# Three padding tiles ahead of the tiles that the tensor engine reads

## The chip, the cores and the metric

The kernel runs on one core of a Trainium2 chip. The metric is the device time of one execution in microseconds (us); the median of a few executions counts. On that core TensorE (PE in the profile) multiplies, with its weight loads listed apart as PEld. VectorE (DVE) and ScalarE (ACT) do the elementwise work, GpSimd (POOL) and SyncE (SP) mostly issue DMAs. A tile lies in the on-chip memory (SBUF) as 128 partitions, and its place is the byte address at which it begins in each partition.

## The reference

```python
q_s = softmax(q, axis=-1)                      # b=8, h=8, s=576, d=64, with 1e-9 in the divisor
k_s = softmax(k, axis=2)                       # over the sequence
kv  = einsum('bhsd,bhse->bhde', k_s, v)
x   = einsum('bhsd,bhde->bhse', q_s, kv)       # then laid out as 4608 tokens x 512
gate = sigmoid(x @ w_gate)                     # 512 x 1536
out  = (gate * (x @ w_val)) @ w_out            # 1536 x 512
```

Linear attention, then a gated feed-forward layer over 4608 tokens, all in float32.

## The kernel before

The tokens are cut in nine windows of 512 (`w` = 0 to 8). Window 0 is computed with plain float32 products (lines 594 and 621) while the weights arrive, are converted, and are cut in a high and a low part. Windows 1 to 8 run in six stages each (`p` = 0 to 5), 48 stages in all, and a stage is `g1(w, p)` and, one stage late, `g2` of the stage before.

`g1` (line 629) forms gate and value of 256 hidden columns with a Strassen-like scheme: seven products `prod`, each of 12 matmuls (two halves `n`, two pieces `kt`, and three pairs of parts: high by high, high by low, low by high). The stationary operand, which the weight load reads, is either `a_w` (the weights, products A11, A12, A22) or `s_sb` (sums of the weights, products S1 to S4). The moving operand is always `c_hl`, 256 columns. So a stage has 36 matmuls with `a_w` and 48 with `s_sb`, all on line 639, all 128x128 by 128x256 in the `float32r` type:

```python
        prod(y, wa(A11), B11, True, False)
        nc.scalar.copy(out=sg[:, 0], in_=y)
        prod(z, wsum(S1), T1, True, False)
        nc.scalar.copy(out=sg[:, 2], in_=z)
        more(S1)
        prod(y, wsum(S2), T2, False, False)
```

`a_w` stays in SBUF for all windows. `s_sb` is one tile: each of its quarters is read by a product, and is then filled again from DRAM by a DMA that GpSimd issues (line 260). `g2` (line 694, matmuls on line 702) multiplies `h` (stationary) by `wo_hl` (moving, 512 columns), 24 matmuls in a stage, and sums over the six stages of a window in PSUM; `wo_hl` too is loaded again in each stage (line 208).

The attention of the next window is woven into the stages: `k_mm` (line 362, plain float32) in stage 2, and `x_mm` (line 522) in stage 4, which multiplies `kv_sb` (stationary) by `ring` tiles (moving). `x_mm` has the same triples of parts as `prod`, and cuts its 512 columns in two where a window crosses from one batch to the next, so that its matmuls have 64 to 512 columns.

The order of the instructions on each engine is that in which the code is written (`tc.manual_schedule()`). Tiles get their places by pools, one after the other in the order in which pools are opened, and within a pool in the order in which tags are first used:

```python
    const = ctx.enter_context(tc.tile_pool(name="const", bufs=1))
    apool = ctx.enter_context(tc.tile_pool(name="apool", bufs=1))
    two = ctx.enter_context(tc.tile_pool(name="two", bufs=2))
    four = ctx.enter_context(tc.tile_pool(name="four", bufs=4))
    ring = ctx.enter_context(tc.tile_pool(name="ring", bufs=11))
```

The first pool, `const`, starts behind some small constants at byte 1152, which is 128 past a multiple of 512. Its big tiles, and the two `kt` tiles of 2304 bytes together, are multiples of 512 long, so they keep that remainder (only the second `kt`, which TensorE does not read, has another), and so does `ident`, 512 bytes long. Behind `ident` come four small tiles (`q_m`, `kmax_0`, `q_r`, `k_r0`: 320 bytes with their rounding), after which `apool` and `two` start with the remainder 448. The last tiles of `two` are six small ones (`k_max`, `k_neg`, `k_sum`, 192 bytes), after which `four` and `ring` have the remainder 128 again.

| tile | read by | role | start, remainder by 512 bytes |
|---|---|---|---|
| `s_sb` | L639 | stationary | 128 |
| `a_w` | L639 | stationary | 448 |
| `c_hl` | L639 | moving | 448 |
| `h` | L702 | stationary | 448 |
| `wo_hl` | L702 | moving | 448 |
| `kv_sb` | L522 | stationary | 128 |
| `ring` | L522 | moving | 128 (384 for a cut at an odd multiple of 64 columns) |

Every slice that these lines take of their tiles starts a multiple of 512 bytes behind the tile's start, but for the cut `ring` slices of the last row.

Of the kernel before, what the change touches and what calls it, by code (L numbers as in the profile page):

```python
# [8 lines left out]
F32 = mybir.dt.float32  # L9
# [8 lines left out]
P = 128  # L18
# [33 lines left out]
def attn_moe(ctx: ExitStack, tc: tile.TileContext, qf, qn, qT, k, kT, v, wg, wv, wo, out):  # L52
    nc = tc.nc

    const = ctx.enter_context(tc.tile_pool(name="const", bufs=1))
    apool = ctx.enter_context(tc.tile_pool(name="apool", bufs=1))
    two = ctx.enter_context(tc.tile_pool(name="two", bufs=2))
    four = ctx.enter_context(tc.tile_pool(name="four", bufs=4))
    ring = ctx.enter_context(tc.tile_pool(name="ring", bufs=11))
    dpool = ctx.enter_context(tc.tile_pool(name="dpool", bufs=2, space=bass.MemoryType.DRAM))  # L60
# [2 lines left out]
    ps_gv = ctx.enter_context(tc.tile_pool(name="ps_gv", bufs=3, space=bass.MemoryType.PSUM))  # L63
    ps_at = ctx.enter_context(tc.tile_pool(name="ps_at", bufs=1, space=bass.MemoryType.PSUM))

    s_sb = const.tile([P, 4, 2, 2, 2 * P], F32R, name="s_sb")
    x_32 = const.tile([P, NP, T], F32, name="x_32")
    sg = const.tile([P, 4, 2, HT], F32, name="sg")
# [12 lines left out]
    )  # L81
    ident = const.tile([P, P], F32, name="ident")
    make_identity(nc, ident)

    ctx.enter_context(tc.manual_schedule())

# [992 lines left out]
```

## Time and profile before

| | us |
|---|---|
| median of 3 runs | 1014.23 (1014.09 to 1016.1) |
| profiled execution, its own time | 1016.99 |
| its span, first to last instruction | 1015.2 |
| PE busy | 957.5 (94%) |
| PEld busy | 826.2 (81%) |
| DVE busy | 611.1 (60%) |
| ACT busy | 475.9 (47%) |

The profiled execution's own time is 1.8 us over its span, and 2.8 us over the median of the runs. In a list by time the first column is the start, the second the time to the group's last end. Matmuls overlap, so one of them lasts far longer (some 280 ns) than the distance to the next; what a matmul costs is that distance, which is the start of the next group less the start of this one, divided by the count. That distance is called the pitch below.

### The profile page before, as it was taken

The numbers are of one execution on the slowest core, as the hardware profiler recorded it, in microseconds if no ns is written. First come the engines' busy times: TensorE is split into PE (matmuls) and PEld (weight loads), VectorE is DVE, ScalarE is ACT, GpSimd is POOL, SyncE is SP. The second block draws the span as 40 slices with busy tenths as digits, with TensorE's granted clock in tenths as the row PEclk, the third lists the DMA queues.
The fourth block names the chain that finished last, engine by engine and source line by source line (L and its number), as shares of the span: only waits on it lengthen the run. The fifth ranks groups of instructions, "written<-read, shape, count | busy, mean of one in ns | idle before, by whom it ended". The sixth has DMA issues, their size and how long they took to land.

```text
span 1015.2 us, 15663 instructions
## 1 busy us (share of the span) xinstructions
PE 957.5 (94%) x6062; PEld 826.2 (81%) x6062; DVE 611.1 (60%) x1010; ACT 475.9 (47%) x815; POOL 171.2 (17%) x323
## 2 busy tenths in 40 slices
PE   5959899878899999999999999999999999999998
PEld 4525344468799999999999999999999999999997
DVE  8476967566266656666666656665665475464342
ACT  3639887345154535363446344633463344353222
POOL 0000001121112211211122111211221122212120
PEclk8979999979799999999999999999999999999999
DMA  9837756889569996899699968996999679868672
GB/s 334 320 106 272 267 222 172 309 266 339 153 207 208 371 322 205 230 365 313 199 248 358 310 200 262 353 300 203 277 340 275 214 203 340 244 184 249 205 208 83
DMA packets 94873, 259.88 MB, mean 256 GB/s; under 512 B 15376, under 2 KB 17680, under 8 KB 94160
## 3 DMA queue, kind: packets, MB, share of 16 engines
q0 software_dynamic: 44720, 170.42, 54.7%
q1 hardware_dynamic: 50080, 88.48, 29.3%
q8 instruction: 48, 0.79, 0.4%
q14 instruction: 25, 0.20, 0.1%
HBM read 230.29 MB, written 28.56 MB: 255 GB/s over the span
## 4 chain that ended last, share of the span: by engine, by line
PE 76%; DMA 8%; ACT 8%; DVE 5%; issue 3%; POOL 1%; SPq 0%; POOLq 0%; DVEq 0%; ACTq 0%
PE gv L639 43%; PE acc L702 22%; PE gv L594 3%; PE at L362 3%; DMA kmax_row<-k_max 2%; PE acc L621 2%; PE gv L522 2%; ACT ring L341 1%; DMA s<-s_sb 1%; ACT ring L441 1%; DMA q_m_row<-q_m 1%; DMA ring<-v_in 1%; DMA ring<-qT_in 1%; ACT kt L295 1%; DMA q_b<-q_m_row 1%
## 5 line engine op out<-in xcount | busy, mean ns | idle before, releaser
L639 PE MATMUL gv<-c_hl,s_sb 128*128 128x256 f32 x2304 | 283.0, 278 | 12.3 <-ACT sg L657 12.2
L639 PEld LDWEIGHTS gv<-c_hl,s_sb 128*128 128x128 f32 x2304 | 272.5, 189 | 14.7 <-ACT sg L657 14.1
L702 PE MATMUL acc<-wo_hl,h 128*128 128x512 f32 x1152 | 272.8, 393 | 0.0
L702 PEld LDWEIGHTS acc<-wo_hl,h 128*128 128x128 f32 x1152 | 214.7, 189 | 43.7 <-issue 0.2
L639 PE MATMUL gv<-c_hl,a_w 128*128 128x256 f32 x1728 | 231.9, 284 | 0.0
L639 PEld LDWEIGHTS gv<-c_hl,a_w 128*128 128x128 f32 x1728 | 220.2, 192 | 4.1 <-issue 1.0
L260 POOL DMA_DIRECT2D s_sb<-s x192 | 102.2, 533 | 327.1 <-PE gv L639 321.5
L665 DVE TENSOR_TENSOR sg<-gv,sg 128x512 f32<-128x512 f32 x48 | 33.2, 691 | 177.7 <-PE gv L639 177.7
L208 POOL DMA_DIRECT2D wo_hl<-wo x96 | 51.1, 533 | 310.4 <-PE acc L702 307.7
L594 PE MATMUL gv<-x,f_w 128*128 128x512 f32 x160 | 72.7, 607 | 9.5 <-ACT h L602 5.6
L667 ACT COPY sg<-gv 128x512 f32<-128x512 f32 x48 | 28.2, 587 | 107.0 <-PE gv L639 107.0
L657 ACT COPY sg<-gv 128x512 f32<-128x512 f32 x48 | 28.0, 584 | 97.7 <-PE gv L639 73.3
L594 PEld LDWEIGHTS gv<-x,f_w 128*128 128x128 f32 x160 | 30.4, 194 | 47.4 <-issue 34.4
L669 DVE TENSOR_TENSOR sg<-sg 128x512 f32<-128x512 f32 x48 | 33.2, 693 | 57.1 <-ACT sg L667 57.1
L621 PE MATMUL acc<-wo_t,h 128*128 128x512 f32 x96 | 47.3, 639 | 14.1 <-DVE h L606 14.1
L690 DVE TENSOR_TENSOR h<-sg,h 128x1024 fp32r<-128x1024 f32 x48 | 58.8, 1226 | 1.6
L672 ACT ACTIVATE sg<-sg 128x512 f32<-128x512 f32 x48 | 30.4, 632 | 54.0 <-DVE sg L671 54.0
L678 DVE TENSOR_TENSOR sg<-sg 128x512 f32<-128x512 f32 x48 | 33.2, 693 | 33.5 <-ACT sg L672 33.5
L621 PEld LDWEIGHTS acc<-wo_t,h 128*128 128x128 f32 x96 | 19.3, 205 | 40.4 <-issue 23.8
L662 ACT COPY sg<-gv 128x512 f32<-128x512 f32 x48 | 28.2, 587 | 44.4 <-PE gv L639 44.4
L659 ACT COPY sg<-gv 128x512 f32<-128x512 f32 x48 | 28.1, 586 | 26.1 <-PE gv L639 26.0
L396 ACT CAST kv_sb<-kmax_b 64x256 fp32r<-64x256 f32 x14 | 5.7, 404 | 66.5 <-DVE kmax_b L372 66.1
(155 smaller groups left out, 1056.1 us busy)
## 6 DMA issues: line engine op xcount, KB each, us to landing
s_sb<-s POOLq DMA_DIRECT2D x192, 512.0 KB, 7.1
wo_hl<-wo POOLq DMA_DIRECT2D x96, 512.0 KB, 5.7
s<-s_sb POOLq DMA_DIRECT2D x5, 2048.0 KB, 8.1
out<-x SPq DMA_DIRECT2D x36, 256.0 KB, 8.8
ring<-k_in SPq DMA_DIRECT2D x28, 256.0 KB, 14.3
ring<-qn_in SPq DMA_DIRECT2D x28, 256.0 KB, 10.4
q_b<-q_m_row SPq DMA_DIRECT2D x56, 128.0 KB, 8.7
ring<-qT_in SPq DMA_DIRECT2D x28, 256.0 KB, 9.0
```

The costliest lines, as they stand in the source:

```text
L208: nc.gpsimd.dma_start(out=t.rearrange("p h e -> p (h e)"), in_=wo_dram[2 * p + i].bitcast(F32R))
L260: nc.gpsimd.dma_start(out=s_sb[:, i].rearrange("p h n e -> p (h n e)"), in_=s_dram[p][:, i * n:(i + 1) * n].bitcast(F32R),)
L362: nc.tensor.matmul(kvps[b][:, hp], lhsT=kt[:n, sl], rhs=vt[:n, sl], start=(t == 0 and hp == 0), stop=(t == len(KTILES) - 1 and hp == NP - ...
L594: nc.tensor.matmul(ps[n], lhsT=w[:, kt // 2, sl], rhs=x_0[:, kt], start=(kt == 0), stop=(kt == NK - 1),)
L621: nc.tensor.matmul(acc[0][m], lhsT=h_0[j][:, m * P:(m + 1) * P], rhs=wo_t[j // 2][:, j % 2], start=(j == 0), stop=(j == NJ - 1),)
L639: nc.tensor.matmul(ps[:, n], lhsT=lh(kt), rhs=c_hl[i][:, x, kt], start=(first and n == 0 and kt == 0 and lh is wh and x == 0), stop=(last ...
L665: nc.vector.tensor_tensor(out=sg[:, 0], in0=rr, in1=sg[:, 0], op=ALU.add)
L669: nc.vector.tensor_tensor(out=sg[:, 3], in0=sg[:, 3], in1=sg[:, 2], op=ALU.add)
L672: nc.scalar.activation(sg[:, 0:2, 0], sg[:, 0:2, 0], AF.Sigmoid)
L678: tt(out=sg[:, 0:2, 0], in0=sg[:, 0:2, 0], in1=sg[:, 0:2, 1], op=ALU.mult)
L690: nc.vector.tensor_tensor(out=lo, in0=sg[:, :, 0], in1=hi.bitcast(F32), op=ALU.subtract)
L702: nc.tensor.matmul(acc[w][m], lhsT=h[lh][:, i, sl], rhs=o[i][:, rh], start=(p == 0 and i == 0 and lh == 0 and rh == 0), stop=(p == NS - 1 ...
```

## The change

```diff
@@ attn_moe
     two = ctx.enter_context(tc.tile_pool(name="two", bufs=2))
+    pad = ctx.enter_context(tc.tile_pool(name="pad", bufs=1))
+    pad.tile([P, 80], F32, name="pad_2")
     four = ctx.enter_context(tc.tile_pool(name="four", bufs=4))
...
+    const.tile([P, 96], F32, name="pad_0")
     s_sb = const.tile([P, 4, 2, 2, 2 * P], F32R, name="s_sb")
...
     make_identity(nc, ident)
+    const.tile([P, 48], F32, name="pad_1")
```

Nothing reads or writes the new tiles. `pad_0` has 384 bytes and stands ahead of `s_sb`: 128 + 384 = 512, so the tiles of `const` start at remainder 0. `pad_1` has 192 bytes and joins the 320 of the small tiles: 320 + 192 = 512, so `apool` and `two` start at remainder 0. `pad_2` has 320 bytes and joins the 192 at the end of `two`: 192 + 320 = 512, so `four` and `ring` start at remainder 0. All tiles of the table above then have the remainder 0 (the cut `ring` slices 256). Each engine has the same instructions in the same order as before, with the same waits; the addresses alone differ. Lines behind the pool list move down by 2 to 5 (line 639 becomes 644, line 702 becomes 707).

## Prediction

> **What bounds the kernel now.** I read the page's busy times first, then the main loop alone by windows, then what PE waited for there.
>
> ```profile
> span 1015.2 us, 15663 instructions
> PE 957.5 (94%) x6062; PEld 826.2 (81%) x6062; DVE 611.1 (60%) x1010; ACT 475.9 (47%) x815; POOL 171.2 (17%) x323
> ...
> 400.00:500.00 100.00, 99.45 (x708) 93.04 (x707) 63.10 (x105) 46.31 (x86) 19.16 (x36) 1.00 0.96 277
> 500.00:600.00 100.00, 99.57 (x714) 93.29 (x713) 63.63 (x107) 46.33 (x86) 19.16 (x36) 1.00 0.97 281
> ...
> PE gv L639 <- ACT sg L657: 2.1, 5, 0.4
> ```
>
> In the windows the columns are PE, PEld, DVE, ACT and POOL busy, the granted clock, the DMA share and GB/s. PE is busy for 99.5 of 100 us at a full clock, and the last row, from the waits after 300 us, has 2.1 us in all for which PE stood still. So the loop is bound by PE's stream of matmuls, and a nanosecond more or less in each is paid in full. DMA engines are 96% occupied, but nothing waits for them in that loop beyond those 2.1 us.
>
> What does a matmul cost? One undisturbed stage in the list by time of PE:
>
> ```profile
> 945.03 1.60 PE L639 MATMUL gv<-c_hl,a_w 128*128 128x256 f32 x12
> 946.47 2.88 PE L639 MATMUL gv<-c_hl,s_sb 128*128 128x256 f32 x24
> 949.19 1.60 PE L639 MATMUL gv<-c_hl,a_w 128*128 128x256 f32 x12
> 950.63 2.88 PE L639 MATMUL gv<-c_hl,s_sb 128*128 128x256 f32 x24
> 953.35 1.60 PE L639 MATMUL gv<-c_hl,a_w 128*128 128x256 f32 x12
> 954.79 5.63 PE L702 MATMUL acc<-wo_hl,h 128*128 128x512 f32 x24
> 960.25 1.60 PE L639 MATMUL gv<-c_hl,a_w 128*128 128x256 f32 x12
> ```
>
> From start to start: 12 matmuls with `a_w` take 1.44 us, 120 ns each; 24 with `s_sb` take 2.72 us, 113.3 ns each; 24 on line 702 take 5.46 us, 227.5 ns each. The stage takes 15.22 us. The reader is to see the first two numbers: the same line, shape, type and moving tile, yet 6.7 ns apart. Both stationary slices are 128 contiguous words of the same layout. What differs is where they start: `s_sb` at remainder 128 of 512 bytes, `a_w` at 448, against `c_hl` at 448. The means in the page's groups say the same less sharply:
>
> ```profile
> L639 PE MATMUL gv<-c_hl,s_sb 128*128 128x256 f32 x2304 | 283.0, 278 | 12.3 <-ACT sg L657 12.2
> L639 PE MATMUL gv<-c_hl,a_w 128*128 128x256 f32 x1728 | 231.9, 284 | 0.0
> ```
>
> A third pair of tiles tells which property counts. `x_mm` reads `kv_sb` at 128 and `ring` at 128, here once in pieces of 256 and once of 512 columns:
>
> ```profile
> 500.31 2.31 PE L522 MATMUL gv<-ring,kv_sb 128*128 128x256 f32 x18
> 502.46 0.88 PE L522 MATMUL at<-ring,kv_sb 128*128 128x256 f32 x6
> 503.18 1.59 PE L639 MATMUL gv<-c_hl,a_w 128*128 128x256 f32 x12
> ...
> 896.43 2.21 PE L522 MATMUL gv<-ring,kv_sb 128*128 128x512 f32 x9
> 898.48 0.84 PE L522 MATMUL at<-ring,kv_sb 128*128 128x512 f32 x3
> 899.16 1.59 PE L639 MATMUL gv<-c_hl,a_w 128*128 128x256 f32 x12
> ```
>
> Its 256-column matmuls take 2.15/18 = 119 and 0.72/6 = 120 ns, its 512-column ones 2.05/9 = 228 and 0.68/3 = 227 ns. So a stationary tile at 128 isn't fast as such: with the moving tile at 128 too it costs the same 120 as 448 against 448. Equal remainders give 120 and 227, at 128 as at 448; the unequal pair gives 113. I read it as two streams out of the same memory, the moving columns and the next weight load, that get in each other's way more often where they start in step.
>
> **The change, part by part.** It adds no instruction, wait or byte of traffic, so no time is paid for the padding itself. It moves addresses, and with them three things.
>
> First, `s_sb` against `c_hl` goes from 128 against 448 to 0 against 0: the one pair with unequal remainders becomes equal. I price its pitch at that of the equal pairs, 120 ns (119.7 over the rows with `a_w`, 1.43 or 1.44 us for 12). That is 119.7 - 113.3 = 6.4 ns more, times 48 matmuls in a stage 0.31 us, times 48 stages 14.7 us.
>
> Not all of it reaches the end. In the first stage part of the loop runs at half clock:
>
> ```profile
> 212.19 2.29 PE L639 MATMUL gv<-c_hl,a_w 128*128 128x256 f32 x12
> 214.32 2.99 PE L639 MATMUL gv<-c_hl,s_sb 128*128 128x256 f32 x24
> ...
> 914.37 1.60 PE L639 MATMUL gv<-c_hl,a_w 128*128 128x256 f32 x12
> 915.81 3.11 PE L639 MATMUL gv<-c_hl,s_sb 128*128 128x256 f32 x24
> 918.75 1.60 PE L639 MATMUL gv<-c_hl,a_w 128*128 128x256 f32 x12
> ...
> 346.61 2.60 ACT ring L341 x5
> 349.21 1.52 ACT kt L295 x4
> 350.73 0.48 ACT sg L657
> ```
>
> There 12 matmuls with `a_w` took 2.13 us, 178 ns each, and the stage begins behind a wait besides (9.6 of the 12.2 us in the group's row above), so I take the whole stage off: 0.3 us. In the first stage of the windows (915.81) the 24 matmuls with `s_sb` already take 2.94 us against 2.72: a short wait, and a slower pitch behind it. The third stages have such a wait too, behind the exponentials of the attention (the last three rows, from the chain of waits). A PE that reaches these waits later, by 12 matmuls x 6.4 ns = 0.08 us since the chain on ACT started, waits so much less, and the disturbed half behind the wait has less to lose: about 0.15 us in each of 13 stages (the first of windows 2 to 8, the third of windows 1 to 6), 2 us. What is left: 14.7 - 0.3 - 2 = 12.4 us.
>
> Second, the pairs that had equal remainders keep them: 448/448 and 128/128 become 0/0 (the cut `ring` slices 0/256). That is 1728 matmuls with `a_w`, 1152 on line 702 and 180 on line 522, and I price them at nothing. No row has a pair at 0/0, so that is bounded from both sides. Downwards by the rival below (a remainder of 0 might be better than all that the trace has). Upwards by 1 ns in each of these 3060, 3 us, since the pitches at 128 and at 448 (119 to 120; 226.7 to 228) lie no further apart. For `s_sb` the bounds are 117.5 (the disturbed half in the rows at 915.81, 2.94 us less a wait of some 0.2, lies near there) and 121: 9 to 17 us before the deductions.
>
> The Trainium skill, in "TensorE: Matmul & The Clock Gate", section "Part 2: What happens when you issue a matmul", says that TensorE has two independent read ports and that loading the next tile's weights takes no read bandwidth from the running matmul. By it no address could matter, the sum would be 0 and the time 1014, against 12.4 and 1027 by the rows. The 120 against 113.3 ns of this trace disagree with it, unless they have another cause than the addresses, which is the second rival.
>
> Third, all other engines' operands move, by multiples of 64 bytes, and so do the DMAs' targets in SBUF. DVE is busy 63% of the loop and ACT 46%, so a few per cent there would hide behind PE; DMA landings would have to grow by more than the stage of slack that the filling of `s_sb` has, since each quarter is asked for as soon as it is read and needed a stage, some 14 us, later:
>
> ```profile
> s_sb<-s POOLq DMA_DIRECT2D x192, 512.0 KB, 7.1
> ```
>
> It lands 7.1 us after its issue. A slower PE leaves more time for it, not less. Cost: nothing.
>
> The sum against the profiled execution: span 1015.2 + 12.4 = 1027.6, its own time 1016.99 + 12.4 = 1029.4. The median of the runs is 2.8 us below that execution, so 1014.23 + 12.4 = 1026.6, and I say 1027. The stage would take 15.22 + 0.31 = 15.5 us.
>
> **The rivals.** *The remainder itself decides, and 0 is the good one* (faster). Suppose that a read which starts at a multiple of 512 bytes saves something that no tile has now. The place is every matmul of lines 639, 702 and 522, and it decides if the pitch of `a_w` falls under 113 ns. For its price, rows in which weight load and moving columns don't disturb each other:
>
> ```profile
> 186.59 7.03 PE L594 MATMUL gv<-x,f_last 128*128 128x512 f32 x16
> 193.46 3.60 PE L621 MATMUL acc<-wo_t,h 128*128 128x512 f32 x8
> ...
> 358.37 1.95 PE L362 MATMUL at<-v,ring 128*128 128x128 f32 x16
> 360.15 3.04 PE L362 MATMUL at<-f_last,ring 128*128 128x128 f32 x24
> ```
>
> A plain float32 pass moves its columns at half the rate: 6.87/16 = 429 ns for 512 columns, so at full rate 215; and 1.78/16 = 111 ns for 128 columns with a weight load each. With 111 and 215 as floors the stage saves 36 x 9 + 48 x 2 + 24 x 12.5 = 0.72 us, 48 stages 35 us: 980. A milder form has the stationary side alone gain, as if 128 were good and 448 bad there and 0 good: `a_w` at 113.3 saves 36 x 6.4 = 0.23 us in a stage, 11 us in all: 1003, or some 996 if line 702 gains as much in each matmul. For it speaks that the slower of the two tiles on line 639 is the one further from a round address, and that nothing in the trace lies at 0. Against it: `kv_sb` lies at 128 like `s_sb` and costs 120, so the moving side would have to be worse at 128 than at 448 by the same 6.4 ns, two effects that cancel by chance. Also, by remainders of 128 bytes the trace has 0 against 64 fast, 64 against 64 and 0 against 0 slow, and the change makes 0 against 0.
>
> *Addresses don't decide* (the same). The 6.4 ns may hang on another property of `s_sb`: it is filled by DMAs, while `a_w` was written by ACT and DVE, and it lies lowest in the memory. Then all pitches stay and the time is 1014. For it speaks that three pairs of tiles are few. Against it: `ring` and `wo_hl` differ in that way too (written by engines, loaded by DMAs) and still both have the slow pitch.
>
> *More of the slower pitch is absorbed* than I took off: only if something else ended the stages. With PE idle for 2.1 us in all after 300 us, at most those 2 us more can go there: 1025, inside the forecast's own range.
>
> **How the numbers follow.** The forecast, slower by an own range of 9 to 18 us (1022 to 1032; the low end is 117.5 ns less the deductions, the high end 121 ns with 3 us on the other pairs), has 0.72. Addresses don't matter: 0.09. The remainder 0 is good: 0.19, of which the milder form 0.11 and the full one 0.08. The range 1011 to 1033 holds the first two, 0.81, and leaves out the faster cases. The measurement of this kernel tells about 0.2% (2 us) from no change, so faster 0.19, same 0.09, slower 0.72.
>
> **What would show it.** In the list by time of the changed kernel, a stage near its end: 24 matmuls with `s_sb` in 2.87 us (right), 2.72 (addresses don't decide), 2.66 (0 is good). Those with `a_w` stay at 1.44 us for 12, those on line 707 at 5.46 us for 24. In the groups, the mean of `s_sb` rises from 278 to about 284 ns. The forecast is wrong if the pitch of `a_w` or of line 707 moves by over 2 ns, or if `s_sb` stays at 113.

## The result and the profile after

| | before | changed |
|---|---|---|
| median of 6 runs, us | 1014.16 (1012.21 to 1019.4) | 1025.22 (1024.38 to 1030.88) |
| ratio, with its 95% interval | | 1.0116 (1.0081 to 1.015) |
| profiled execution: span | 1015.2 | 1023.1 |
| PE busy | 957.5 | 967.8 |

The change makes the kernel 11 us slower. The lines of the changed kernel's page that answer to those shown of before:

```profile
span 1023.1 us, 15663 instructions
PE 967.8 (95%) x6062; PEld 837.2 (82%) x6062; DVE 611.1 (60%) x1010; ACT 476.0 (47%) x815; POOL 170.6 (17%) x323
...
L644 PE MATMUL gv<-c_hl,s_sb 128*128 128x256 f32 x2304 | 295.6, 284 | 11.2 <-ACT sg L662 11.2
...
L644 PE MATMUL gv<-c_hl,a_w 128*128 128x256 f32 x1728 | 232.3, 284 | 0.0
...
s_sb<-s POOLq DMA_DIRECT2D x192, 512.0 KB, 6.6
```

DVE and ACT are busy for the same time to 0.1 us. Of the two groups of the products' line (639 before, 644 now) one has moved: the mean matmul with `s_sb` went from 278 to 284 ns, that with `a_w` stayed at 284. One undisturbed stage in the list by time of PE:

```profile
951.63 1.60 PE L644 MATMUL gv<-c_hl,a_w 128*128 128x256 f32 x12
953.06 3.04 PE L644 MATMUL gv<-c_hl,s_sb 128*128 128x256 f32 x24
955.94 1.60 PE L644 MATMUL gv<-c_hl,a_w 128*128 128x256 f32 x12
957.38 3.04 PE L644 MATMUL gv<-c_hl,s_sb 128*128 128x256 f32 x24
960.26 1.60 PE L644 MATMUL gv<-c_hl,a_w 128*128 128x256 f32 x12
961.70 5.63 PE L707 MATMUL acc<-wo_hl,h 128*128 128x512 f32 x24
967.17 1.60 PE L644 MATMUL gv<-c_hl,a_w 128*128 128x256 f32 x12
```

From start to start, 24 matmuls with `s_sb` take 2.88 us, 120 ns each, where they took 2.72 (113.3). The 12 with `a_w` take 1.43 or 1.44 us and the 24 on line 707 take 5.47 us, as before. The stage is 15.54 us long instead of 15.22.

Where the time went is best read from the fourth stage on, since what lies ahead of it varies from one execution to the next. Its first row in the list by time, of the kernel before:

```profile
268.10 1.59 PE L639 MATMUL gv<-c_hl,a_w 128*128 128x256 f32 x12
```

and of the changed kernel:

```profile
264.13 1.59 PE L644 MATMUL gv<-c_hl,a_w 128*128 128x256 f32 x12
```

From there to the end the profiled executions take 1015.2 - 268.1 = 747.1 and 1023.1 - 264.1 = 759.0 us: 11.9 us more, in 45 stages. The changed kernel's execution came to that stage 4 us sooner, so its span is only 7.9 us longer. 45 stages at 0.32 us would make 14.4 us: some 2.5 of them did not reach the end, in the stages in which PE waits or in which the pitch behind a wait had been slower before.

### The profile page after: what moved, and what is told of

It is laid out like the page before. It is cut to its first block, busy times and chain, and to the rows that moved or that the text cites. A ratio compares the mean times of both kernels' runs of the same rounds, so it can differ in the third digit from the quotient of the medians.

```text
span 1023.1 us, 15663 instructions
## 1 busy us (share of the span) xinstructions
PE 967.8 (95%) x6062; PEld 837.2 (82%) x6062; DVE 611.1 (60%) x1010; ACT 476.0 (47%) x815; POOL 170.6 (17%) x323
## 4 chain that ended last, share of the span: by engine, by line
PE 77%; DMA 8%; ACT 8%; DVE 3%; issue 2%; POOL 0%; SPq 0%; POOLq 0%; ACTq 0%; DVEq 0%
PE gv L644 45%; PE acc L707 23%; PE at L367 3%; PE gv L599 3%; DMA kmax_row<-k_max 2%; PE acc L626 2%; PE gv L527 2%; ACT ring L346 2%; ACT ring L446 1%; DMA s<-s_sb 1%; DMA lent<-v_in 1%; ACT kt L300 1%; DMA lent<-kT_in 1%; DMA ring<-qf_in 1%; ACT L446 1%
## 5 line engine op out<-in xcount | busy, mean ns | idle before, releaser
L644 PE MATMUL gv<-c_hl,s_sb 128*128 128x256 f32 x2304 | 295.6, 284 | 11.2 <-ACT sg L662 11.2
L644 PEld LDWEIGHTS gv<-c_hl,s_sb 128*128 128x128 f32 x2304 | 285.2, 192 | 12.8 <-ACT sg L662 12.6
L670 DVE TENSOR_TENSOR sg<-gv,sg 128x512 f32<-128x512 f32 x48 | 33.2, 692 | 191.3 <-PE gv L644 191.3
L676 DVE TENSOR_TENSOR sg<-gv,sg 128x512 f32<-128x512 f32 x48 | 33.2, 692 | 6.2
```

Of the source, the lines that this page charges most:

```text
L644: nc.tensor.matmul(ps[:, n], lhsT=lh(kt), rhs=c_hl[i][:, x, kt], start=(first and n == 0 and kt == 0 and lh is wh and x == 0), stop=(last ...
L670: nc.vector.tensor_tensor(out=sg[:, 0], in0=rr, in1=sg[:, 0], op=ALU.add)
L676: nc.vector.tensor_tensor(out=sg[:, 1], in0=z, in1=sg[:, 1], op=ALU.add)
```

## The experiments

In what follows the *distance* of a pair is the start of the moving tile less that of the stationary one, by remainders of 512 bytes. `s_sb` has the distance 320 before (448 less 128) and 0 after. Pitches are read as above, from start to start. A mean over the loop is that of the single starts from the fourth stage on, with the gaps of waits left out (some 2,100 of them for `s_sb`, 1,600 for `a_w`, 1,100 for line 702). A mean counts the slower matmuls next to other lines and to waits too, so that of line 702 lies at 228.3 where an undisturbed stage has 227.5.

**Is it the multiple of 512, or the distance?** The first run leaves the change as it is but for `s_sb` and `kv_sb`, which it puts at remainder 64 (the first padding tile is in fact 64 bytes longer, and the second 64 shorter). In this run and in all that move `s_sb`, the other tiles of `const` behind it move along; of the pairs in the table of the tiles, that changes `kv_sb` with `ring` beside `s_sb` with `c_hl`, and no other.

```diff
-    const.tile([P, 96], F32, name="pad_0")
+    const.tile([P, 112], F32, name="pad_0")
...
-    const.tile([P, 48], F32, name="pad_1")
+    const.tile([P, 32], F32, name="pad_1")
```

> The changed kernel with the first padding tile 64 bytes shorter: s_sb and kv_sb start at remainder 64, all other tiles of the tensor engine stay at 0. Theory (the distance between the start of the moving tile and that of the stationary one decides, by remainders of 128 bytes; 64 apart is fast, 0 apart is slow): s_sb falls from 120 to about 113.5 ns a matmul although it leaves the multiple of 512, a_w stays at 120 and the 512-column matmuls at 227, kv_sb with ring falls from 120 to about 113 at 256 columns; the time returns to that of the kernel before, 1012 to 1017 us. Rival 1 (what made s_sb fast before was its own remainder 128, or the moving tile's 448): s_sb stays at 120 and the time at 1025. Rival 2 (s_sb differs by something else than its address): stays at 120 too.

Measured: ratio to the kernel before 1.0045 (1.0029 to 1.0061), so more than half of the loss is gone, but not all. A stage, list by time of PE:

```profile
951.64 1.59 PE L643 MATMUL gv<-c_hl,a_w 128*128 128x256 f32 x12
953.08 2.99 PE L643 MATMUL gv<-c_hl,s_sb 128*128 128x256 f32 x24
955.90 1.60 PE L643 MATMUL gv<-c_hl,a_w 128*128 128x256 f32 x12
```

24 matmuls with `s_sb` take 2.82 us: 117.5 ns each. `s_sb` left the multiple of 512, `a_w`, `c_hl`, `h` and `wo_hl` stayed, and it became faster: the rival that puts its speed down to something other than its address falls. That its own remainder counts, and not the distance, is not settled by this run. And it was to be 113.5. If the distance counts, then not only by remainders of 128: 448 is 64 by that measure, as 320 is. The matmuls of `x_mm` with 256 columns, whose distance became 448 too, also missed the 113 that was expected: the 18 on `gv` take 2.12 us, 117.8 ns each, where they took 119.

The control for the multiple of 512 puts `s_sb` of the kernel before at 448, with the tiles of `const` behind it, and leaves `a_w`, `c_hl`, `h`, `wo_hl` and `ring` at their remainders. The distance is 0 as in the change, and no tile that the tensor engine reads starts at a multiple of 512.

```diff
+    const.tile([P, 80], F32, name="pad_0", bufs=1)
     s_sb = const.tile([P, 4, 2, 2, 2 * P], F32R, name="s_sb")
...
     make_identity(nc, ident)
+    const.tile([P, 48], F32, name="pad_1", bufs=1)
```

> The kernel before with s_sb and kv_sb at remainder 448, all else where it was: c_hl less s_sb is 0, and no tile that the tensor engine reads starts at a multiple of 512 bytes. Theory (the distance decides): s_sb 120 ns as in the changed kernel, a_w 120, line 702 unchanged, the loop's stage 15.54 us against 15.22, ratio 1.010 to 1.014. Rival (the multiple of 512 itself was what cost in the changed kernel): s_sb 113 to 118, ratio 1.000 to 1.005.

Measured: ratio 1.0116 (1.0096 to 1.0135), the change's own number.

```profile
952.60 1.59 PE L641 MATMUL gv<-c_hl,a_w 128*128 128x256 f32 x12
954.04 3.04 PE L641 MATMUL gv<-c_hl,s_sb 128*128 128x256 f32 x24
956.92 1.60 PE L641 MATMUL gv<-c_hl,a_w 128*128 128x256 f32 x12
```

2.88 us for 24, 120 ns. The multiple of 512 neither costs nor gains anything; the equal remainder costs the 11 us.

**Which distances are fast?** With the layout of the change, `s_sb` and `kv_sb` were put at 192, 448 and 320, which are the distances 320, 64 and 192 (`pad_0` of 16, 80 and 48 words, with `pad_1` so that all else stays at 0).

```diff
-    const.tile([P, 96], F32, name="pad_0")
+    const.tile([P, 16], F32, name="pad_0", bufs=1)
...
-    const.tile([P, 48], F32, name="pad_1")
```

> The changed kernel with s_sb and kv_sb at remainder 192 and all others at 0, so that c_hl less s_sb is 320 as in the kernel before, while both tiles start elsewhere than there. Theory, mended after the run with s_sb at 64 (the distance by 512 decides, and of the distances 64, 192, 320, 448 each has its own pitch): s_sb 113.5 ns, a_w 120, 512 columns 227, time as before the change (ratio 0.998 to 1.002). Rival (the own remainders count: 128 with 448 was a lucky pair): s_sb stays near 118 as with 64, ratio 1.004.

> The changed kernel with s_sb and kv_sb at remainder 448: c_hl less s_sb is 64. Theory: a pitch of its own for this distance, near the 117.6 ns that 64 gave in another layout. Rival (any odd multiple of 64 gives 113 or 118 by chance of the entry): 113 in some stages and 118 in others.

> The changed kernel with s_sb and kv_sb at remainder 320: c_hl less s_sb is 192. In another layout, entered from a pitch of 113 to 118, this distance gave now 113 and now 118. Theory: entered from a_w at 120 it settles on one of the two in all stages. Rival: it changes from stage to stage as there.

Measured: 320 bytes away again, though at other addresses, the ratio is 0.9981 (0.9964 to 0.9998), so the loss is gone. The list by time of that run, first the start of its fourth stage (1012.2 - 264.85 = 747.4 us to the end, against 747.1 before), then a product of sums and what follows it:

```profile
264.85 1.60 PE L642 MATMUL gv<-c_hl,a_w 128*128 128x256 f32 x12
...
958.67 2.88 PE L642 MATMUL gv<-c_hl,s_sb 128*128 128x256 f32 x24
961.39 1.60 PE L642 MATMUL gv<-c_hl,a_w 128*128 128x256 f32 x12
```

The same two rows of the run with distance 64:

```profile
960.50 2.88 PE L643 MATMUL gv<-c_hl,s_sb 128*128 128x256 f32 x24
963.23 1.60 PE L643 MATMUL gv<-c_hl,a_w 128*128 128x256 f32 x12
```

And of the run with distance 192:

```profile
963.59 2.99 PE L643 MATMUL gv<-c_hl,s_sb 128*128 128x256 f32 x24
966.42 1.60 PE L643 MATMUL gv<-c_hl,a_w 128*128 128x256 f32 x12
```

2.72, 2.73 and 2.83 us for 24. The runs with distances 64 and 192 are of one execution each (1015.83 and 1019.55 us beside a median of 1017.38 for the kernel before). So 320 and 64 give 113.3 to 113.8 ns, 448 and 192 give 117.5 to 117.9 (by the means 114.0, 113.8, 117.7 and 117.8): the distance counts by remainders of 256, 64 fast and 192 slower, where the stream comes in from 12 matmuls of `a_w` at distance 0. The theory's guess for 64, its own pitch near 117.6, missed. With these runs the last rival on the addresses falls, that the tile's own remainder decides: `s_sb` at 448 takes 120 ns against `c_hl` at 448, in the control, and 113.8 against `c_hl` at 0.

**Other pairs.** Three runs of one execution each, with padding that sets several pairs at once:

```diff
+    const.tile([P, 64], F32, name="pad_1", bufs=1)
...
     x_0 = apool.tile([P, NP, T], F32, name="x_0", tag="c2")
+    apool.tile([P, 96], F32, name="pad_2", bufs=1)
...
     lent = {i: lend(i) for i in (0, 2, 3, 4, 5)}
+    apool.tile([P, 32], F32, name="pad_3", bufs=1)
...
     load_w(2)
+    apool.tile([P, 96], F32, name="pad_4", bufs=1)
+    two.tile([P, 16], F32, name="pad_6", bufs=1)
```

The diff is that of the first of them. In the second the five tiles have 56, 104, 24, 104 and 8 words, in the third 96, 16, 112, 16 and 80.

> The kernel before with padding that sets other distances, moving less stationary, by remainders of 512: c_hl less s_sb 64, c_hl less a_w 128, wo_hl less h 64. Theory: s_sb about 113.5 ns, a_w 120, the 512-column matmuls fall from 227 to about 221, so about 1152 x 6 ns = 7 us less than before: 1007. Rival (only the distance 320 that the kernel before had is fast): s_sb 120 and line 702 at 227, 1027 us. Rival (each tile's own remainder decides): a_w at 64 and s_sb at 128 with c_hl at 192 give pitches other than 113.5 and 120.

> The kernel before with padding, distances c_hl less s_sb 32, c_hl less a_w 96, wo_hl less h 32. The theory has no row for a distance of 32 or 96 by 128. If the pitch runs evenly from 0 to 64, s_sb and a_w lie near 117 and line 702 near 224, and the time near 1014 + 8 - 5 - 3 = 1014 us. If only a distance of exactly 64 helps, all are slow: 120 and 227, 1027 us. If any distance but 0 helps fully, 113.5, 113.5 and 221: 1014 - 11 - 7 = 996 us.

> The kernel before with padding, distances c_hl less s_sb 192, c_hl less a_w 448 (that is -64), wo_hl less h 320. All three are 64 by remainders of 128. Theory: s_sb stays at 113.5, a_w falls from 120 to 113.5 (1728 x 6.4 ns = 11 us), line 702 from 227 to about 221 (7 us): 996 us. If the distance counts by 256 or 512 instead, the three differ from each other: those at 192 and 448 equal that at 320 by 256 only in part (320 is 64 by 256, the other two 192), so a_w and s_sb would differ from the 113.5 of before.

The times, 1024.95, 1024.95 and 1020.44 us beside a median of 1017.92 for the kernel before, are of one execution each, so the pitches are read (means over the loop, ns):

| run | `s_sb`: distance, pitch | `a_w`: distance, pitch | line 702: distance, pitch |
|---|---|---|---|
| before | 320, 113.8 | 0, 119.8 | 0, 228.3 |
| changed | 0, 120.0 | 0, 119.8 | 0, 228.4 |
| first of the three | 64, 117.6 | 128, 118.8 | 64, 229.9 |
| second | 32, 116.9 | 96, 119.7 | 32, 233.6 |
| third | 192, 116.2 | 448, 116.2 | 320, 230.0 |

Three things that were expected did not come. `s_sb` at distance 64 has 117.6 ns and not 113.5, here where `a_w` ahead of it is at 128. The 512-column matmuls of line 702 do not gain from an unequal distance, they lose: 24 take 5.60 us at distance 32, where they take 5.46 at 0. From the second run, where line 702 is 704:

```profile
946.05 5.76 PE L704 MATMUL acc<-wo_hl,h 128*128 128x512 f32 x24
951.65 1.60 PE L641 MATMUL gv<-c_hl,a_w 128*128 128x256 f32 x12
```

And the third run has no pitch at all that goes with its distances: 118 in some stages, 113 in others, with nothing different in the remainders. Its stage at 650 us (the line number is 641, the second group of `s_sb` comes behind a wait):

```profile
649.39 1.57 PE L641 MATMUL gv<-c_hl,a_w 128*128 128x256 f32 x12
650.80 1.58 PE L641 MATMUL gv<-c_hl,s_sb 128*128 128x256 f32 x12
652.75 1.65 PE L641 MATMUL gv<-c_hl,s_sb 128*128 128x256 f32 x12 [0.38 <-ACT sg L659]
654.23 1.52 PE L641 MATMUL gv<-c_hl,a_w 128*128 128x256 f32 x12
655.59 2.88 PE L641 MATMUL gv<-c_hl,s_sb 128*128 128x256 f32 x24
658.31 1.52 PE L641 MATMUL gv<-c_hl,a_w 128*128 128x256 f32 x12
```

12 with `a_w` take 1.41 us ahead of the wait and 1.36 behind it, and the 24 with `s_sb` that follow 2.72. What the pitch goes with is what ran ahead: nearly all stages that come in from the 512-column matmuls begin at 118 and leave it only behind a wait, if at all, while six of the seven stages behind `x_mm` run at 113.

**One distance, two pitches.** That suggests two steady pitches for a pair whose tiles stand an odd multiple of 64 bytes apart, 113 and 118, and that a stream keeps the one it came in with until something disturbs it. The next run gives both stationary tiles of `g1` the fast distance 320.

```diff
     two = ctx.enter_context(tc.tile_pool(name="two", bufs=2))
+    two.tile([P, 80], F32, name="pad_5", bufs=1)
...
+    apool.tile([P, 48], F32, name="pad_2", bufs=1)
...
+    apool.tile([P, 80], F32, name="pad_3", bufs=1)
...
+    apool.tile([P, 48], F32, name="pad_4", bufs=1)
```

> The kernel before with a_w moved to remainder 128 too, so that both stationary tiles of g1 stand 320 from c_hl; h and wo_hl stay at 448. Theory: all 84 matmuls of a stage at 113.5, 36 x 6.4 ns = 0.23 us less in a stage, 11 us in all, ratio 0.989. Rival (there are two steady pitches at this distance, 113 and 118, and which one is taken hangs on how the stream comes in; before, s_sb came in behind 12 matmuls at 120): some or all stages settle at 118, then 84 matmuls at 118 against 36 at 120 and 48 at 113.5: 0.14 us more in a stage, 7 us, ratio up to 1.007.

Measured: ratio 1.0035 (1.0017 to 1.0052), the rival's side. An ordinary stage, and one in which a wait of 0.1 us falls into the stream of `s_sb`:

```profile
604.36 1.60 PE L641 MATMUL gv<-c_hl,a_w 128*128 128x256 f32 x12
605.79 2.99 PE L641 MATMUL gv<-c_hl,s_sb 128*128 128x256 f32 x24
608.62 1.58 PE L641 MATMUL gv<-c_hl,a_w 128*128 128x256 f32 x12
...
619.72 1.58 PE L641 MATMUL gv<-c_hl,a_w 128*128 128x256 f32 x12
621.13 3.12 PE L641 MATMUL gv<-c_hl,s_sb 128*128 128x256 f32 x24
624.09 1.52 PE L641 MATMUL gv<-c_hl,a_w 128*128 128x256 f32 x12
625.45 2.88 PE L641 MATMUL gv<-c_hl,s_sb 128*128 128x256 f32 x24
628.17 1.52 PE L641 MATMUL gv<-c_hl,a_w 128*128 128x256 f32 x12
```

At the top 24 matmuls with `s_sb` take 2.83 us, 118 ns each. In the lower stage the stream comes in alike (1.41 us for the first 12), loses some 0.1 us in its first group of 24, and leaves it at another pitch: 1.36 us for 12 and 2.72 for 24, to the end of the stage. Same addresses, same instructions, two pitches. This is the first stage of a window, and the first stages of all windows read and write at the same addresses; each has such a wait, and of the seven from window 2 on two go to 113 behind it and five stay at 118. What sets the two apart from the five is not known. So what the kernel before got for `s_sb` hung on two things: the distance, and the 12 matmuls of `a_w` at distance 0 ahead of each pair of `s_sb` products, from which a stream nearly always goes to 113. In two of the 45 stages, both behind a wait, the pair behind A12 took 118 there too.

If so, products may be moved to the fast pitch as long as the first of a stage keeps the distance 0. The first try moves six of the seven by gaps in and between the `c_hl` tiles, the second only the last product, by 64 bytes ahead of its `c_hl` tile.

First (with two more padding tiles of 48 words that, like those shown, put `a_w` and the `c_hl` tiles in place):

```diff
+            if i == T2:
+                flat_t = apool.tile([P, 8 * HT + 16], F32R, name="c_hl", tag="c1")
+                for x in (T2, B21):
+                    o = (x - T2) * (4 * HT + 16)
+                    c_hl[x] = flat_t[:, o:o + 4 * HT].rearrange("p (x k t) -> p x k t", x=2, k=2)
...
     make_identity(nc, ident)
+    const.tile([P, 64], F32, name="pad_0", bufs=1)
...
     load_w(0)
+    apool.tile([P, 16], F32, name="pad_1", bufs=1)
```

Second:

```diff
     load_w(0)
+    apool.tile([P, 16], F32, name="pad_0", bufs=1)
...
     load_wo(0)
+    apool.tile([P, 112], F32, name="pad_1", bufs=1)
```

> The kernel before with paddings inside and between the c_hl tiles, so that the first product of a stage (A11) has the distance 0 and the six others 64 or 320. Theory (at these distances there are two steady pitches, 113 and 118; a stream that comes in from 12 matmuls at distance 0 takes 113 and keeps it until it is disturbed): A11 120 ns, the other 72 matmuls 113.5 in the stages without a wait, so that A12 and A22 save 24 x 6.4 = 0.15 us there; in the 13 stages with a wait behind S1 all that follows may settle at 118 and lose 48 x 4.5 = 0.2 us. Over 48 stages 5.4 less 2.8 = about 3 us less than before, ratio 0.995 to 1.000. Rival (the distance alone sets the pitch, and the run with both stationary tiles at 320 was at 118 for another reason): six products at 118, ratio 1.003.

> The kernel before with one of the c_hl tiles, that of the last product of a stage (T4 for A22), 64 bytes further: distance 64, the others as before (A11 and A12 at 0, the sums at 320). Theory: the last 12 matmuls of a stage come in from 113.5 and keep it: 12 x 6.4 ns = 0.08 us in each of 48 stages, 3.7 us, ratio 0.9964. Rival: they settle at 118, 12 x 2 ns x 48 = 1 us, ratio 0.999.

Measured: ratios 0.9992 (0.9977 to 1.0007) and 0.9963 (0.9945 to 0.9981). A stage of the first in the list by time:

```profile
945.23 1.60 PE L646 MATMUL gv<-c_hl,a_w 128*128 128x256 f32 x12
946.66 2.88 PE L646 MATMUL gv<-c_hl,s_sb 128*128 128x256 f32 x24
949.38 1.53 PE L646 MATMUL gv<-c_hl,a_w 128*128 128x256 f32 x12
950.75 2.99 PE L646 MATMUL gv<-c_hl,s_sb 128*128 128x256 f32 x24
953.58 1.57 PE L646 MATMUL gv<-c_hl,a_w 128*128 128x256 f32 x12
954.99 5.64 PE L709 MATMUL acc<-wo_hl,h 128*128 128x512 f32 x24
```

And of the second:

```profile
954.93 1.59 PE L639 MATMUL gv<-c_hl,a_w 128*128 128x256 f32 x12
956.36 2.88 PE L639 MATMUL gv<-c_hl,s_sb 128*128 128x256 f32 x24
959.08 1.60 PE L639 MATMUL gv<-c_hl,a_w 128*128 128x256 f32 x12
960.52 2.88 PE L639 MATMUL gv<-c_hl,s_sb 128*128 128x256 f32 x24
963.24 1.52 PE L639 MATMUL gv<-c_hl,a_w 128*128 128x256 f32 x12
964.60 5.63 PE L702 MATMUL acc<-wo_hl,h 128*128 128x512 f32 x24
```

In the first, the stream comes in at 113 and keeps it through A12 (1.37 us for 12, 114 ns). With the third product of sums it falls to 118 (2.83 for 24) and stays there (1.41 for 12). It does so in every stage without a wait, where the theory had it only behind a wait; so the ratio lies in the theory's range, but this step of it was wrong. What stands at that place is a change of both tiles at once, after which the last moving slice of A12 lies 384 bytes from the next weights; at the change from S2 to A12, which the pitch came through unchanged, that was 256. That this is the cause was not tried. In the second, the last 12 matmuls take 1.36 us instead of 1.44, as expected, the stage is 15.14 us long, and the kernel is faster than the kernel before, by 3.7 us in the medians (1014.72 against 1018.46 of that comparison). Some of the gain goes back into waits behind the evacuation on ACT, 3.3 us after 300 us where there were 2.1 (from what PE waited for):

```profile
PE gv L639 <- ACT sg L657: 3.3, 7, 0.5
```

## Why the prediction was right

It forecast 1027 us, 12.4 more than before; measured 1025.2, 11.1 more in the medians, and 11.9 more in the loop of the two profiled executions. The ratio's interval, 1.0081 to 1.015, is 8 to 15 us, so the 2 us between forecast and measurement say nothing. By its steps:

- *PE's stream bounds the loop, and each nanosecond is paid.* Right: the undisturbed stage grew by 15.54 - 15.22 = 0.32 us, against 0.31 forecast, and no other engine's busy time changed.
- *`s_sb` goes from 113.3 to the pitch of the equal pairs, 119.7.* Right, at 120; the controls with the distance 320 elsewhere (0.9981) and 0 elsewhere (1.0116) show that the distance is what did it. The argument for it was that pairs with equal remainders are slow whatever the remainder, and the runs at 0/0 and at 448/448 bear that out.
- *The deductions, 0.3 and 2 us.* The second is right in kind and near in size: some 2.5 us from the fourth stage on. What PE waited for after 300 us fell from 2.1 to 1.7 us (the row stands below this list), and the stages with a wait grew by less: the first one of the last window took 929.81 - 914.37 = 15.44 us before and 936.09 - 920.47 = 15.62 after. The 0.3 for the first stage can't be told from what varies there.
- *The other pairs at nothing.* Right: 1.44 us for 12 with `a_w`, 5.47 for 24 on line 707.
- *The range.* Its low end doesn't come out of its own terms: 117.5 ns is 9.7 us before the deductions and 7.4 after them, which gives the 1022 but not the 9.
- *The rivals.* That 0 is the good remainder falls with the changed kernel itself: at 0 against 0 no pitch is below those of before. That addresses don't decide falls with the runs that move `s_sb` and leave `a_w` and `c_hl` alone. That more is absorbed by waits, at 1025, is not told apart by the time; what PE waited for fell by 0.4 us of 2.1, and not to nothing. The Trainium skill's statement in "TensorE: Matmul & The Clock Gate" (section "Part 2: What happens when you issue a matmul"), that a weight load takes no read bandwidth from the running matmul, does not fit these runs: moving the stationary tile by 320 bytes, with its pool, costs 0.16 us in 24 matmuls. That it is read bandwidth which is lost, no run shows.
- *What was too simple.* The argument that sorted the three pairs by remainders of 128 gave the right sign, but it isn't the rule: at distances 192 and 448 the pitch was 117.5 to 117.9 and not 113. And the "disturbed half" behind a wait, priced as a nuisance of 117.5 ns, was the second steady pitch that such a pair can have.

The waits of the changed kernel after 300 us:

```profile
PE gv L644 <- ACT sg L662: 1.7, 5, 0.4
```

Why a pair in step is slower, and why there are two pitches, is not shown: no record tells of a memory access. "Two streams out of the same memory" remains a reading: it would have 256 columns slow at distance 0, as they are, but doesn't say why 64 and 192 differ, why one address has two pitches, or why 512 columns are best at distance 0.

## What to carry to other kernels

Where a matmul's weight load and its moving columns both come at full rate, compare the pitches of lines that differ in nothing but their tiles: 6% of the pitch hung here on where two tiles stand to each other, and nothing on a round address. Padding for alignment's sake can put tiles in step that stood well; for matmuls of 256 columns it is worth trying a distance of 64 bytes, one pair at a time, and reading the pitch from start to start in an undisturbed stage. A pitch can also depend on what ran ahead, so the time of a pair in one place is no promise for another: moving both stationary tiles of `g1` to the good distance at once made the kernel slower (1.0035).

## What the runs showed of the hardware that was not expected

- 128x256 matmuls in `float32r`, each with its own weight load, run at 120 ns where moving and stationary tile start at the same remainder by 512 bytes (0/0 and 448/448 on line 639), and at 113.3 or 118 where they stand an odd multiple of 64 apart; entered from a stream at 120, distances of 64 and 320 nearly always took 113, distances of 192 and 448 took 118.
- Such a stream keeps its pitch across products and tiles; a wait moved it from 118 to 113 in some stages (0.1 us, with both tiles at 320; most of that run's waits left it at 118), or, in the kernel before, from 113 to about 118 (the rows at 915.81).
- 128x512 matmuls cost 228.3 ns at distance 0, 229.9 at 64, 230.0 at 320 and 233.6 at 32 (means over the loop; the last three of one execution each, which set other pairs too).
